# Bucketed attention and a feed-forward on one core: mask products over 64 rows, hashes in four column groups, squares on ScalarE, and weights converted in place

## The chip, the cores and the metric

The kernel runs on one core of a Trainium2 chip. Five engines work side by side, each with an instruction queue of its own that it takes in order: PE (TensorE, matrix products; PEld are its weight loads), DVE (VectorE), ACT (ScalarE), POOL (GpSimd) and SP (SyncE, which issues the DMAs here). They meet through semaphores. PE and the others exchange data through PSUM, which has eight banks for each partition; everything else lies in SBUF. The metric is device time in microseconds. Before the change the median of three runs is 1216.94 us (1216.66 to 1217.87).

## What is computed

```python
# q, k, v: (4, 8, 768, 64); proj: (64, 6)
q_bucket = sum of (q @ proj > 0) * 2**bit          # 6 bits a token
k_bucket = the same of k
mask = q_bucket[..., :, None] == k_bucket[..., None, :]
scores = where(mask, (q @ k.T) / 8, -1e9)
attn = softmax(scores); x = attn @ v               # (4, 8, 768, 64)
x = x.transpose(0, 2, 1, 3).reshape(3072, 512)
h = x @ w_in                                       # (512, 2048), float64 input
g = maximum(h, 0) + alpha * minimum(h, 0)
out = g @ w_out                                    # (2048, 512)
```

## The kernel before

There are two functions. `fast_path` computes everything on the assumption that exponents can't overflow, and writes a flag; `general_path` runs only if the flag says so. With this data it doesn't run, and it isn't changed.

`fast_path` works on **pairs** of heads: 4 batches of 4 pairs, the two heads of a pair side by side in the partitions 0 to 63 and 64 to 127. A **unit** is one pair and one half (384) of its queries, so there are 32 units, `u` = 0 to 31, and a unit has four **slots**. The scores are made transposed: a key tile of 128 keys by 384 queries for each head, six key tiles `kc` a unit, two in each of the slots 0, 2 and 3 (a **part**).

- `turn` transposes q and k of the next pair on PE (`tp_q`, `tp_k`), and ACT copies them to `qT`, `kT`. `magnitude` reduces those to a maximum and a minimum (`mags`, L548, DVE); `verdict` makes the flag of them at the end.
- `hash_bits` multiplies qT and kT by the projection (`hs`, L561, PE): q into the PSUM rows 0 to 63 and k into 64 to 127, each with the bits of both heads. Four DVE instructions a half (L565, L567) make of it the bit tiles `qb` and `kb`, 12 rows for each head: 6 bits and their complements, `kb` scaled so that their product is large and negative where the buckets differ.
- `scores` adds for each head that mask product (12 rows, bf16) and the product of qT and kT (64 rows, f32, which PE does in two passes) in PSUM (`sc`, L578). ACT makes exponentials of them (`pt`, L583), and the sum over the six key tiles is made in `acc` (L591): on POOL, and in the first batch for `kc` 4 and 5 on DVE.
- `attend` (slot 0 of the next unit) multiplies with v (`av`, L598); `divide` (slot 2) sums `acc` over its partitions with a product by ones (`sm`, L615) and divides: two DVE instructions (L619, L620), the reciprocal (L621), and on POOL a product (L622) and a sum (L623) into `xT`.
- The weights come as 8-byte floats. `round_weight` makes f32 of a block of 128 x 1024: ACT takes an absolute value (L521), DVE has five instructions (L522, L523, L526, L527, L530), between which ACT has another one (L528) and POOL an addition (L529). There are 16 blocks, two a unit in the units 0 to 7. The first feed-forward work (`h`, `neg`, `g`) belongs to unit 9 by the program.
- The feed-forward of a batch (`ff1`: `h`, L632, and `neg`, `g` on DVE; `ff2`: `z`, L648) is cut into the slots of the eight units that follow the batch's attention.

The program is written as one loop over units and slots, but the order of each engine's queue is set by a scheduler that goes by its own estimate of when each operand is ready, so an instruction can stand far from its place in the program. PSUM tiles named `sc`, `mi` and `ff` have two buffers each.

Of the kernel before, what the change touches and what calls it, by code (L numbers as in the profile page):

```python
# [348 lines left out]
def kernel(  # L349
# [31 lines left out]
    flag = const_flag = None  # L381
# [10 lines left out]
def fast_path(  # L392
# [12 lines left out]
    nc = tc.nc  # L405
# [15 lines left out]
    SAFE = 80.0 / SCALE / D  # L421
# [5 lines left out]
    psum = ctx.enter_context(tc.tile_pool(name="ps", bufs=2, space=bass.MemoryType.PSUM))  # L427

# [7 lines left out]
    wh = const.tile([P, D], F32, name="wh")  # L436
# [5 lines left out]
    mags = const.tile([P, 2, 2 * NPAIR], F32, name="mags")  # L442
# [3 lines left out]
    NPT = 9  # L446
# [4 lines left out]
    prob, acc, av, vmean, xT = {}, {}, {}, {}, {}  # L451

    def load(pi, names):
        b, hp = pairs[pi]
        for name, src in names:
            if name == "v":
                t = pool.tile([P, 2, NC * D], F32, name=f"vn{pi}", tag="vn", bufs=3)
                nc.sync.dma_start(t, src[b, 2 * hp : 2 * hp + 2].rearrange("h (p c) d -> p h (c d)", c=NC))
            else:
                t = pool.tile([P, NC, 2, D], F32, name=f"{name}n{pi}", tag=f"{name}n")  # L460
                for s in range(2):
                    nc.sync.dma_start(t[:, :, s], src[b, 2 * hp + s].rearrange("(p c) d -> p c d", c=NC))
# [8 lines left out]
    def setup():  # L471


        nc.vector.memset(wh, 0.0)
        for s in range(2):
            nc.sync.dma_start(wh[D * s : D * s + D, 32 * s : 32 * s + NB], proj)
# [3 lines left out]
        for s in range(2):  # L480
            r = slice(D * s, D * s + D)
            nc.vector.tensor_copy(wh[r, 32 * s + NB : 32 * s + 2 * NB], wh[r, 32 * s : 32 * s + NB])
        for t, inner, outer in ((cq, 0.5, 0.0), (tk, 0.0, -3.0e38), (mk, 2.0 * BIG, -BIG)):
            nc.vector.memset(t, 0.0)
            for r in range(0, P, 32):
                nc.vector.memset(t[r : r + 2 * NB], outer)
                nc.vector.memset(t[r : r + NB], inner)
        for t in pts:
# [11 lines left out]
    def load_weight(i):  # L500
        dst, src, j = views[i // 2]
        half = i % 2
        if src is moe_w_in:
            w = DFF // 4
            view = src[half * DM // 2 : (half + 1) * DM // 2, j * w : (j + 1) * w]
        else:
            w = DFF // 8
            view = src[(2 * j + half) * w : (2 * j + half + 1) * w]
        raw[i] = wpool.tile([P, 2, 512], src.dtype, name=f"raw{i}", tag="raw")
        nc.sync.dma_start(raw[i], view.rearrange("(o p) f -> p o f", p=P))  # L510

    def round_weight(i):
# [3 lines left out]
        words = raw[i].bitcast(U32).rearrange("p o (f t) -> p o f t", t=2)  # L516
        lo, hi = words[:, :, :, 0], words[:, :, :, 1]
        dst = views[i // 2][0][:, 2 * (i % 2) : 2 * (i % 2) + 2]
        x = wpool.tile([P, 2, 512], F32, name=f"wx{i}", tag="wx")
        r = wpool.tile([P, 2, 512], F32, name=f"wr{i}", tag="wr")  # L520
        nc.scalar.activation(x, hi.bitcast(F32), AF.Abs)  # L521
        nc.vector.tensor_scalar(x, x, HI_MIN, HI_MAX, op0=ALU.max, op1=ALU.min)  # L522
        nc.vector.tensor_scalar(  # L523
            x.bitcast(U32), x.bitcast(U32), 3, 0x40000000, op0=ALU.logical_shift_left, op1=ALU.bitwise_xor,
        )
        nc.vector.tensor_scalar(r.bitcast(U32), x.bitcast(U32), 0x7F800000, None, op0=ALU.bitwise_and)  # L526
        nc.vector.scalar_tensor_tensor(r, lo, 2.0 ** -52, r, op0=ALU.mult, op1=ALU.mult)  # L527
        nc.scalar.activation(x, x, AF.Abs)  # L528
        nc.gpsimd.tensor_tensor(r, x, r, op=ALU.add)  # L529
# [5 lines left out]
    def turn(pi, name, half):  # L535
# [4 lines left out]
        for i in range(CH):  # L540
            nc.tensor.transpose(ps[:, i * P : (i + 1) * P], src[:, CH * half + i], ident)  # L541
        nc.scalar.copy(tr[name, pi][:, half * CW : (half + 1) * CW], ps)  # L542

    def magnitude(pi, name):

        n = "qk".index(name)
        for i, op in enumerate((ALU.max, ALU.min)):
            nc.vector.tensor_reduce(  # L548
                mags[:, n, 2 * pi + i : 2 * pi + i + 1], tr[name, pi], axis=mybir.AxisListType.X, op=op,
            )  # L550

    def hash_bits(pi, half):


        if half == 0:
            for name in "qk":
# [232 lines left out]
```

## Time and profile before

| | |
|---|---|
| median of the runs | 1216.94 us |
| the profiled execution | 1216.79 us, span 1215.0 us |
| PE busy | 1132.4 us (93%) |
| DVE busy | 527.1 us (43%) |
| POOL busy | 364.3 us (30%) |
| ACT busy | 243.3 us (20%) |
| mean granted clock of PE | 0.956 |
| longest PE groups | `h` 344.3 us, `z` 339.0 us, `sc` product 188.8 us, `av` 142.4 us |

Shares of the whole span hide that the stages differ. The page's slices, each a fortieth of the span, and the busy times by stage show where which engine is full. A row of a group gives the line, the engine, the operation, what it writes and reads, partitions x elements, the count, the busy time, the mean length of one, and the idle time of the engine just before them with what ended it. PE's matrix products are pipelined, so the length of one says less than the distance between two starts.

### The profile page before, as it was taken

The page shows a single profiled execution, that of the slowest core. Times are in us where ns is not written, and L with a number is a line of the kernel's source. Part 1 is how long each engine was busy: PE and PEld are TensorE (multiplying, and loading weights), DVE is VectorE, ACT ScalarE, POOL GpSimd, SP SyncE. Part 2 cuts the span into 40 slices and gives each one's busy share as a digit, 9 for nine tenths or more (in the row PEclk, how much of TensorE's full clock was granted, in tenths as well). Part 3 has the DMA queues.
Part 4 walks back from the last instruction along what each step waited for, and adds up shares of the span by engine and source line. Part 5 has one row for each costly group of instructions (what it writes and reads, how often), then busy time and mean ns, then how long its engine had stood idle before and what let it go on. Part 6 is the DMA issues. An engine that isn't in the chain of part 4 may idle for free.

```text
span 1215.0 us, 10348 instructions
## 1 busy us (share of the span) xinstructions
PE 1132.4 (93%) x4163; PEld 503.5 (41%) x4163; DVE 527.1 (43%) x697; ACT 243.3 (20%) x345; POOL 364.3 (30%) x239
## 2 busy tenths in 40 slices
PE   7576765999999999999999999999999999999998
PEld 3122221344444444444444444444444444554553
DVE  7889888564313442164313442164313431330320
ACT  4443433222111121212121221222121111000000
POOL 3455556433222332333222332333223331000000
PEclk8777887799999999999999999999999999999999
DMA  7432332101010101000010101000000000000000
GB/s 195 127 124 82 109 96 83 26 13 26 22 35 22 26 13 35 18 13 27 22 35 22 26 13 35 18 14 14 9 9 9 1 1 18 9 1 18 9 9 20
DMA packets 62585, 42.72 MB, mean 35 GB/s; under 512 B 51248, under 2 KB 55360, under 8 KB 62528
## 3 DMA queue, kind: packets, MB, share of 16 engines
q1 hardware_dynamic: 62528, 41.96, 11.9%
q8 instruction: 35, 0.57, 0.2%
q14 instruction: 22, 0.18, 0.1%
HBM read 35.66 MB, written 6.29 MB: 35 GB/s over the span
## 4 chain that ended last, share of the span: by engine, by line
PE 84%; DVE 9%; POOL 3%; issue 3%; ACT 1%; DMA 0%; POOLq 0%; ACTq 0%
PE z L648 28%; PE h L632 27%; PE sc L578 14%; PE av L598 9%; POOL wr L529 3%; PE hs L561 2%; PE sm L615 2%; DVE wx L523 1%; DVE wr L527 1%; DVE wx L522 1%; DVE w_in L530 1%; PE tp_q L541 1%; PE tp_k L541 1%; DVE kb L567 1%; DVE w_out L530 1%
## 5 line engine op out<-in xcount | busy, mean ns | idle before, releaser
L632 PE MATMUL h<-xT,w_in 128*128 128x384 f32 x1024 | 344.3, 489 | 0.0
L648 PE MATMUL z<-w_out,g 128*128 128x512 f32 x768 | 339.0, 595 | 0.0
L591 POOL TENSOR_TENSOR acc<-acc,pt 128x768 f32<-128x768 f32 x112 | 193.6, 1729 | 447.2 <-ACT pt L583 444.0
L632 PEld LDWEIGHTS h<-xT,w_in 128*128 128x128 f32 x1024 | 189.4, 190 | 136.8 <-issue 14.8
L583 ACT ACTIVATE pt<-sc 128x768 f32<-128x768 f32 x192 | 154.9, 811 | 450.3 <-PE sc L578 450.3
L648 PEld LDWEIGHTS z<-w_out,g 128*128 128x128 f32 x768 | 143.2, 190 | 179.4 <-issue 177.3
L637 DVE TENSOR_SCALAR neg<-h,alpha 128x384 f32<-128x384 f32 x128 | 79.1, 618 | 275.0 <-PE h L632 273.0
L578 PE MATMUL sc<-qT,kT 64*128 64x384 f32 x768 | 188.8, 561 | 0.0
L598 PE MATMUL av<-pt,vn 128*64 128x385 f32 x768 | 142.4, 521 | 24.2 <-DVE dn L620 24.2
L578 PE MATMUL sc<-qb,kb 12*128 12x384 bf16 x384 | 70.7, 344 | 38.6 <-DVE kb L567 31.6
L598 PEld LDWEIGHTS av<-pt,vn 128*64 128x64 f32 x768 | 55.6, 146 | 108.9 <-issue 83.0
L591 POOL TENSOR_TENSOR acc<-pt,pt 128x768 f32<-128x768 f32 x32 | 59.3, 1853 | 120.6 <-ACT pt L583 120.6
L578 PEld LDWEIGHTS <-kb 12*128 12x128 bf16 x384 | 19.3, 92 | 152.7 <-issue 117.7
L619 DVE TENSOR_SCALAR al<-sm,vm 128x384 f32<-128x384 f32 x32 | 19.8, 617 | 144.1 <-PE sm L615 143.9
L621 DVE RECIPROCAL dn<-dn 128x384 f32<-128x384 f32 x32 | 81.6, 2551 | 0.9
L578 PEld LDWEIGHTS sc<-qT,kT 64*128 64x128 f32 x768 | 61.5, 193 | 36.0 <-issue 36.0
L548 DVE TENSOR_REDUCE mags<-qT 128x1 f32<-128x768 f32 x32 | 29.2, 945 | 101.5 <-ACT qT L542 101.5
L639 DVE SCALAR_TENSOR_TENSOR g<-h,neg 128x384 f32<-128x384 f32 x128 | 71.2, 556 | 3.9
L654 ACT COPY o<-z 128x512 f32<-128x512 f32 x24 | 14.0, 585 | 265.9 <-PE z L648 265.9
L622 POOL TENSOR_TENSOR dn<-rx,dn 128x384 f32<-128x384 f32 x32 | 36.1, 1128 | 71.8 <-DVE dn L621 71.7
L529 POOL TENSOR_TENSOR wr<-wx,wr 128x1024 f32<-128x1024 f32 x16 | 43.1, 2695 | 37.2 <-DVE wr L527 29.7
L565 DVE TENSOR_SCALAR qb<-hs,cq 12x384 bf16<-12x384 f32 x64 | 37.7, 590 | 37.6 <-PE hs L561 37.1
(59 smaller groups left out, 507.4 us busy)
## 6 DMA issues: line engine op xcount, KB each, us to landing
raw<-in_moe_w_in_dram SPq DMA_DIRECT2D x8, 1024.0 KB, 5.1
raw<-in_moe_w_out_dram SPq DMA_DIRECT2D x8, 1024.0 KB, 4.8
qn<-in_q_dram SPq DMA_DIRECT2D x32, 192.0 KB, 3.9
kn<-in_k_dram SPq DMA_DIRECT2D x32, 192.0 KB, 3.3
vn<-in_v_dram SPq DMA_DIRECT2D x16, 384.0 KB, 3.4
out_dram<-o SPq DMA_DIRECT2D x24, 256.0 KB, 2.0
wh<-in_proj_dram SPq DMA_DIRECT2D x2, 1.5 KB, 3.2
alpha<-in_moe_alpha_dram SPq DMA_DIRECT2D x1, 8.0 KB, 2.5
```

The costliest lines, as they stand in the source:

```text
L529: nc.gpsimd.tensor_tensor(r, x, r, op=ALU.add)
L565: nc.vector.tensor_scalar(bits["q", pi][dst, cols], ps[r], 0.0, cq[r], op0=ALU.is_gt, op1=ALU.subtract)
L578: nc.tensor.matmul(sc[:, s, :CW], what["k", pi][r, ks], what["q", pi][r, qs], start=first, stop=not first,)
L583: nc.scalar.activation(pt[:, :, :CW], sc[:, :, :CW], AF.Exp, scale=SCALE)
L591: eng.tensor_tensor(a, first, pt[:, :, :CW], op=ALU.add)
L598: nc.tensor.matmul(ps[D * s : D * s + D], nat["v", pi][:, s, kc * D : (kc + 1) * D], prob[pi, g, kc][:, s], start=(kc == 0), stop=(kc == N ...
L621: nc.vector.reciprocal(den, den)
L622: nc.gpsimd.tensor_tensor(den, av[pi, g], den, op=ALU.mult)
L632: nc.tensor.matmul(ps, w[:, kk, o : o + P], xT[b][:, kk, ch * CW : (ch + 1) * CW], start=(kk == 0), stop=(kk == NK - 1),)
L637: nc.vector.tensor_scalar(neg, ps, 0.0, alpha[:, f : f + 1], op0=ALU.min, op1=ALU.mult)
L639: nc.vector.scalar_tensor_tensor(g, ps, 0.0, neg, op0=ALU.max, op1=ALU.add)
L648: nc.tensor.matmul(ps, gT[b, ch, f][:, t * P : (t + 1) * P], w_out[part][:, i], start=(f == 0), stop=(f == NF - 1),)
```

## The change

- The bit tiles are zero outside their 12 rows, and the mask product takes 64 rows for each head.
- The hash is made in four column groups of 32 PSUM rows: head 0 q, head 0 k, head 1 q, head 1 k, with two projections `wh` of 32 columns. `qb` is then made in one DVE instruction over 128 rows, `kb` in two over 32 rows. `kb` has two fixed buffers, zeroed once.
- `magnitude` is a Square on ACT with a running sum, in place on the q or k tile, instead of two DVE reductions; the flag's bound is changed to suit.
- Weights are converted in 32 quarters of 128 x 512, in place in `w_in` and `w_out`, with one buffer `wr` and three raw tiles. By the loop there are two quarters a unit in the units 0 to 6 and four a unit from unit 7.
- In the first batch `acc` is three tiles, each the POOL sum of two key tiles, and `divide` adds them with three products by ones. Later batches keep the chain, all of it on POOL.
- `attend` copies into `xT`; the product of the division is on DVE in place of POOL.
- q and k have one buffer each, v two, `pt` eight; the loads of q, k and v are issued later and one by one. The pool of the feed-forward is opened at the start.
- Every product is pinned to program order on PE (`pe`).

```diff
+    pe = tc.keep_in_program_order
-    wh = const.tile([P, D], F32, name="wh")
+    wh = [const.tile([P, 32], F32, name=f"wh{s}") for s in range(2)]
+    kbs = [const.tile([P, S], BF16, name=f"kb{i}") for i in range(2)]
-    NPT = 9
+    NPT = 8
...
     def load_weight(i):
-        raw[i] = wpool.tile([P, 2, 512], src.dtype, name=f"raw{i}", tag="raw")
-        nc.sync.dma_start(raw[i], view.rearrange("(o p) f -> p o f", p=P))
+        raw[i] = wpool.tile([P, 512], src.dtype, name=f"raw{i}", tag="raw", bufs=3)
+        nc.sync.dma_start(raw[i], view)
...
     def round_weight(i):
-        x = wpool.tile([P, 2, 512], F32, name=f"wx{i}", tag="wx")
-        r = wpool.tile([P, 2, 512], F32, name=f"wr{i}", tag="wr")
-        nc.scalar.activation(x, hi.bitcast(F32), AF.Abs)
-        nc.vector.tensor_scalar(x, x, HI_MIN, HI_MAX, op0=ALU.max, op1=ALU.min)
+        r = wpool.tile([P, 512], F32, name=f"wr{i}", tag="wr", bufs=1)
+        nc.scalar.activation(dst, hi.bitcast(F32), AF.Abs)
+        nc.vector.tensor_scalar(dst, dst, HI_MIN, HI_MAX, op0=ALU.max, op1=ALU.min)
...
     def magnitude(pi, name):
-        for i, op in enumerate((ALU.max, ALU.min)):
-            nc.vector.tensor_reduce(
-                mags[:, n, 2 * pi + i : 2 * pi + i + 1], tr[name, pi], axis=mybir.AxisListType.X, op=op,
-            )
+        t = nat[name, pi].rearrange("p c h d -> p (c h d)")
+        nc.scalar.activation(t, t, AF.Square, accum_out=mags[:, n, pi : pi + 1])
     def hash_bits(pi, half):
-        for n, name in enumerate("qk"):
-            nc.tensor.matmul(ps[D * n : D * n + D], wh, tr[name, pi][:, cols], start=True, stop=True)
         for s in range(2):
-            dst = slice(D * s, D * s + 2 * NB)
-            r = slice(32 * s, 32 * s + 2 * NB)
-            nc.vector.tensor_scalar(bits["q", pi][dst, cols], ps[r], 0.0, cq[r], op0=ALU.is_gt, op1=ALU.subtract)
-            r = slice(D + 32 * s, D + 32 * s + 2 * NB)
-            nc.vector.tensor_scalar(bits["k", pi][dst, cols], ps[r], tk[r], mk[r], op0=ALU.is_gt, op1=ALU.mult)
+            for n, name in enumerate("qk"):
+                r = D * s + 32 * n
+                pe(nc.tensor.matmul(ps[r : r + 32], wh[s], tr[name, pi][:, cols], start=True, stop=True))
+        nc.vector.tensor_scalar(bits["q", pi][:, cols], ps, tq, cq, op0=ALU.is_gt, op1=ALU.subtract)
+        for s in range(2):
+            r = slice(D * s + 32, D * s + D)
+            nc.vector.tensor_scalar(
+                bits["k", pi][D * s : D * s + 32, cols], ps[r], tk[r], mk[r], op0=ALU.is_gt, op1=ALU.mult,
+            )
     def scores(pi, g, part):
-            for what, first, rows in ((bits, True, 2 * NB), (tr, False, D)):
+            for what, first in ((bits, True), (tr, False)):
                 for s in range(2):
-                    r = slice(D * s, D * s + rows)
+                    r = slice(D * s, D * s + D)
...
-                eng = nc.vector if pi < NP and kc >= 4 else nc.gpsimd
-                eng.tensor_tensor(a, first, pt[:, :, :CW], op=ALU.add)
+            if kc % 2 == 0 and (kc == 0 or pi < NP):
+                acc.setdefault((pi, g), []).append(pool.tile([P, 2, CW], F32, name=f"acc{pi}_{g}_{kc}", tag="acc", bufs=4))
+            a = acc[pi, g][-1]
+            if kc == 1 or (pi < NP and kc % 2 == 1):
+                nc.gpsimd.tensor_tensor(a, prob[pi, g, kc - 1][:, :, :CW], pt[:, :, :CW], op=ALU.add)
+            elif pi >= NP and kc > 1:
+                nc.gpsimd.tensor_tensor(a, a, pt[:, :, :CW], op=ALU.add)
     def divide(pi, g):
-        for s in range(2):
-            nc.tensor.matmul(ps[D * s : D * s + D], ones, acc[pi, g][:, s], start=True, stop=True)
+        n = len(acc[pi, g])
+        for i, a in enumerate(acc[pi, g]):
+            for s in range(2):
+                pe(nc.tensor.matmul(ps[D * s : D * s + D], ones, a[:, s], start=(i == 0), stop=(i == n - 1)))
...
-        nc.gpsimd.tensor_tensor(den, av[pi, g], den, op=ALU.mult)
+        nc.vector.tensor_tensor(den, den, x, op=ALU.mult)
...
-            if slot % 2 == 0 and 2 * u + slot // 2 < NW:
-                i = 2 * u + slot // 2
+            i = 2 * u + slot // 2 if u < UNITS - 1 else 4 * u + slot - 2 * UNITS + 2
+            if (slot % 2 == 0 or u >= UNITS - 1) and i < NW:
                 round_weight(i)
-                if i + 2 < NW:
-                    load_weight(i + 2)
+                if i + 3 < NW:
+                    load_weight(i + 3)
```

The order of the queues shows what the scheduler makes of it. The rows below have the line, the instruction, what it writes and reads with the tile's number, and the shape. In the changed kernel the lines of a conversion are L531, L532, L535, L536 and L539, in the order of L522 to L530.

DVE in the second pair, before, two blocks of weights after the hash bits:

```order
L567 TENSOR_SCALAR kb_614<-hs_646,tk,mk 12x384
L522 TENSOR_SCALAR wx_675<-wx_675 128x1024
L522 TENSOR_SCALAR wx_727<-wx_727 128x1024
L523 TENSOR_SCALAR wx_675<-wx_675 128x1024
L523 TENSOR_SCALAR wx_727<-wx_727 128x1024
L526 TENSOR_SCALAR wr_676<-wx_675 128x1024
L526 TENSOR_SCALAR wr_728<-wx_727 128x1024
L527 SCALAR_TENSOR_TENSOR wr_676<-raw_555,wr_676 128x1024
L527 SCALAR_TENSOR_TENSOR wr_728<-raw_609,wr_728 128x1024
L530 SCALAR_TENSOR_TENSOR w_out_81<-raw_555,wr_676 128x1024
L548 TENSOR_REDUCE mags<-qT_687 128x1
```

and at the same place of the changed kernel, with quarters:

```order
L535 TENSOR_SCALAR wr_1051<-w_in_84 128x512
L532 TENSOR_SCALAR w_out_85<-w_out_85 128x512
L536 SCALAR_TENSOR_TENSOR wr_1051<-raw_918,wr_1051 128x512
L531 TENSOR_SCALAR w_out_85<-w_out_85 128x512
L532 TENSOR_SCALAR w_out_85<-w_out_85 128x512
L539 SCALAR_TENSOR_TENSOR w_in_84<-raw_918,wr_1051 128x512
L535 TENSOR_SCALAR wr_1081<-w_out_85 128x512
L536 SCALAR_TENSOR_TENSOR wr_1081<-raw_970,wr_1081 128x512
L539 SCALAR_TENSOR_TENSOR w_out_85<-raw_970,wr_1081 128x512
L535 TENSOR_SCALAR wr_1130<-w_out_85 128x512
L536 SCALAR_TENSOR_TENSOR wr_1130<-raw_1027,wr_1130 128x512
L539 SCALAR_TENSOR_TENSOR w_out_85<-raw_1027,wr_1130 128x512
```

Two blocks went abreast through two `wx` and two `wr`; now one quarter follows another through one `wr`, and L539 often stands right behind L536.

DVE of the changed kernel where the conversion ends; `al`, `dn` and `den` belong to the division of the last unit of the first batch, `neg` and `g` to the feed-forward:

```order
L532 TENSOR_SCALAR w_out_88<-w_out_88 128x512
L535 TENSOR_SCALAR wr_1733<-w_out_88 128x512
L536 SCALAR_TENSOR_TENSOR wr_1733<-raw_1604,wr_1733 128x512
L539 SCALAR_TENSOR_TENSOR w_out_88<-raw_1604,wr_1733 128x512
L630 TENSOR_SCALAR al_1_1249<-sm_1_1241,vm_1048 128x384
L631 TENSOR_SCALAR dn_1_1248<-sm_1_1241 128x384
L632 RECIPROCAL dn_1_1248<-dn_1_1248 128x384
L633 TENSOR_TENSOR dn_1_1248<-dn_1_1248,xT_344 128x384
L648 TENSOR_SCALAR neg_0_0_1319<-h_0_0_1314,alpha 128x384
L650 SCALAR_TENSOR_TENSOR g_0_0_1321<-h_0_0_1314,neg_0_0_1319 128x384
```

The last of the 32 quarters stands ahead of the first `neg`, though by the loop the quarters run on into the units with feed-forward.

PE in unit 9, before, where the hash of the next pair stands between scores and feed-forward:

```order
L578 MATMUL sc_1_3_1285<-qb_1077,kb_1078 128x384
L578 MATMUL sc_1_3_1285<-qT_921,kT_1023 128x384 x2
L561 MATMUL hs_1296<-qT_1143,wh 64x384
L561 MATMUL hs_1296<-kT_1223,wh 64x384
L632 MATMUL h_0_3_1303<-xT_387,w_in_77 128x384 x4
L632 MATMUL h_0_4_1312<-xT_387,w_in_78 128x384 x4
L615 MATMUL sm_0_1322<-acc_0_1133,ones 64x384 x2
```

and in the changed kernel:

```order
L587 MATMUL sc_1_3_1381<-qb_1093,kb_79 128x384
L587 MATMUL sc_1_3_1381<-qT_920,kT_1029 128x384 x2
L570 MATMUL hs_1401<-qT_1177,wh_70 32x384
L570 MATMUL hs_1401<-kT_1308,wh_70 32x384
L570 MATMUL hs_1401<-qT_1177,wh_71 32x384
L570 MATMUL hs_1401<-kT_1308,wh_71 32x384
L643 MATMUL h_0_3_1409<-xT_344,w_in_81 128x384 x4
L643 MATMUL h_0_4_1418<-xT_344,w_in_82 128x384 x4
L626 MATMUL sm_0_1427<-acc_0_0_1158,ones 64x384 x2
```

The neighbours are the same, and the hash has four products in place of two.

## What I predicted before the run

> **What bounds the kernel now.** I read the page's slices first, then the busy times by stage, then the DVE groups of the first stage and the PE timeline of the second. Four lines of the page:
>
> ```profile
> span 1215.0 us, 10348 instructions
> ...
> PE   7576765999999999999999999999999999999998
> ...
> DVE  7889888564313442164313442164313431330320
> ...
> PEclk8777887799999999999999999999999999999999
> ```
>
> There are two kernels in one: some eight slices in which DVE is fuller than PE and the granted clock is low, and then PE filled to the end. The busy times by stage (length, then PE, PEld, DVE, ACT, POOL with counts, granted clock, DMA share, GB/s) put the border at 238.3 us, where the feed-forward (`h`) begins in earnest:
>
> ```profile
> 17.60:210.60 193.00, 129.42 (x562) 47.15 (x560) 166.84 (x155) 78.45 (x101) 105.76 (x51) 0.78 0.35 106
> 210.60:238.30 27.70, 22.66 (x90) 8.01 (x91) 17.73 (x21) 7.30 (x11) 12.18 (x8) 0.69 0.11 28
> 238.30:1208.30 970.00, 970.00 (x3482) 443.86 (x3481) 331.77 (x479) 151.98 (x226) 245.43 (x166) 1.00 0.06 17
> ```
>
> From 17.6 to 238.3 us (220.7 us) DVE works 166.84 + 17.73 = 184.6 us and rests 36.1. From 238.3 on PE is busy for 970.00 of 970.00 us at clock 1.00. So two things can shorten the program: less DVE work, or fewer DVE waits, ahead of 238.3; and less time on PE behind it. DVE's groups from 17.6 to 238.3 us (line, engine, operation, shapes, count, busy us, mean ns, idle before):
>
> ```profile
> L527 DVE SCALAR_TENSOR_TENSOR wr<-raw,wr 128x1024 f32<-128x1024 uint32 x16 | 22.2, 1400 | 0.1
> ...
> L530 DVE SCALAR_TENSOR_TENSOR w_in<-raw,wr 128x1024 uint32<-128x1024 uint32 x8 | 19.6, 2457 | 13.8 <-POOL wr L529 13.8
> L530 DVE SCALAR_TENSOR_TENSOR w_out<-raw,wr 128x1024 uint32<-128x1024 uint32 x8 | 18.8, 2353 | 12.3 <-POOL wr L529 12.3
> L523 DVE TENSOR_SCALAR wx<-wx 128x1024 uint32<-128x1024 uint32 x16 | 18.4, 1166 | 0.1
> L522 DVE TENSOR_SCALAR wx<-wx 128x1024 f32<-128x1024 f32 x16 | 17.1, 1081 | 1.3 <-ACT wx L521 1.2
> L591 DVE TENSOR_TENSOR acc<-acc,pt 128x768 f32<-128x768 f32 x16 | 16.3, 1020 | 0.0
> L526 DVE TENSOR_SCALAR wr<-wx 128x1024 uint32<-128x1024 uint32 x16 | 12.2, 778 | 0.1
> L567 DVE TENSOR_SCALAR kb<-hs,tk,mk 12x384 bf16<-12x384 f32 x16 | 10.9, 680 | 0.3
> L565 DVE TENSOR_SCALAR qb<-hs,cq 12x384 bf16<-12x384 f32 x16 | 9.7, 603 | 0.2
> L548 DVE TENSOR_REDUCE mags<-qT 128x1 f32<-128x768 f32 x10 | 9.2, 940 | 7.1 <-ACT qT L542 7.1
> L548 DVE TENSOR_REDUCE mags<-kT 128x1 f32<-128x768 f32 x8 | 7.4, 941 | 0.0
> ```
>
> The conversion of the weights (L522 to L530) is 108.3 us of it. Its two L530 rows also hold 13.8 + 12.3 = 26.1 us of the 36.1 us of rest: DVE waits there for the POOL addition (L529).
>
> **Stage 1: the conversion isn't spread.** The loop asks for two quarter conversions in each of the units 0 to 6 and four afterwards, which would halve DVE's load in the first batch. The order of instructions says otherwise: DVE's rows are not pinned, and all 32 quarters stand ahead of the first `neg` of the feed-forward, some four between one division and the next. So the 108.3 us stay in stage 1. I cost the edits there one by one.
>
> Removed from DVE: the additions into `acc`, 16.3 us, and the `mags` reductions, 9.2 + 7.4 = 16.6 us. The hash bits take three instructions a half where they took four: 20.6 us become 8 halves x (0.60 + 2 x 0.68) = 15.7, so -4.9; I take 128 or 32 rows to cost what 12 rows do, since all have 384 columns. Added: the product in the division moves from POOL to DVE, 8 x 0.51 = 4.1 us (half of an L591 instruction of 1020 ns, which has twice the columns); and 160 conversion instructions of 512 columns in place of 80 of 1024. No row shows how much of an instruction is fixed. The bounds are 0 and 0.1 us each; I take 0.06 x 80 = 4.8. DVE's work is then 184.6 - 16.3 - 16.6 - 4.9 + 4.1 + 4.8 = **155.7 us**.
>
> ```profile
> L529 POOL TENSOR_TENSOR wr<-wx,wr 128x1024 f32<-128x1024 f32 x16 | 43.1, 2695 | 37.2 <-DVE wr L527 29.7 <-ACT pt L583 7.5
> ...
> L632 PE MATMUL h<-xT,w_in 128*128 128x384 f32 x13 | 5.2, 510 | 0.0
> ```
>
> Its rest: `wr` has one buffer now, so the next quarter can't enter it until the last instruction of this one (L539, which was L530) has read it, and that one waits for POOL's addition, 2695 / 2 = 1.35 us. There are twice as many waits of half the length. In some the order puts the next quarter's first two instructions or hash bits, in about half it puts nothing. Bounds: 18 us (half the waits gone) and 62 (all 32 additions fully exposed, 32 x 1.6, and 10 of other rest). I keep the 36.1 of now.
>
> The first conversion starts when the first raw tile has landed; its Abs starts at 16.45 us now:
>
> ```profile
> 16.45 1.11 ACT L521 ACTIVATE wx<-raw 128x1024 f32<-128x1024 f32 x1
> ```
>
> The tile is half as large, so I put the first DVE conversion at 15.5 us instead of 17.6 (bounds 12.5 and 17.6). The feed-forward then begins at 15.5 + 155.7 + 36.1 = 207 us instead of 238.3: **-31 us** (bounds -52 and -3).
>
> What else moves in stage 1 I cost at nothing, for a named cover. The page's group for the Exp:
>
> ```profile
> L583 ACT ACTIVATE pt<-sc 128x768 f32<-128x768 f32 x192 | 154.9, 811 | 450.3 <-PE sc L578 450.3
> ```
>  Two more `sm` pairs in 8 units on PE lie in its 193.00 - 129.42 = 63.6 us of rest. Square on ACT, 10 times about 0.81 us like an Exp over as large a tile, lies in ACT's rest of 193.00 - 78.45 = 114.6 us. The q and k loads with one buffer wait behind Square, but are issued more than a unit ahead of their transposes; only the pair 1 load at the very start is late, where DVE isn't waiting for it. One thing is given back: the scheduler slipped early pieces of `h` into PE's rest, the 13 records above, of which 12 belong to three pieces ahead of their turn. With PE pinned to program order they are paid in stage 2: 12 x 0.33 = **+4 us**. If the cover on PE failed, that is the last rival below.
>
> **Stage 2: the scores.** PE's timeline (start us, us, instruction); a unit issues three such parts of two key tiles each:
>
> ```profile
> 401.41 0.34 PE L578 MATMUL sc<-qb,kb 12*128 12x384 bf16 x2
> 401.67 0.92 PE L578 MATMUL sc<-qT,kT 64*128 64x384 f32 x4
> 402.52 0.34 PE L578 MATMUL sc<-qb,kb 12*128 12x384 bf16 x2
> 402.79 0.92 PE L578 MATMUL sc<-qT,kT 64*128 64x384 f32 x4
> 403.63 0.55 PE L541 MATMUL tp_q<-ident,qn 128*128 128x128 f32 x3
> ...
> 406.69 4.10 PE L598 MATMUL av<-pt,vn 128*64 128x385 f32 x24
> 410.72 0.55 PE L541 MATMUL tp_q<-ident,qn 128*128 128x128 f32 x3
> 411.11 5.33 PE L632 MATMUL h<-xT,w_in 128*128 128x384 f32 x16
> 416.37 0.34 PE L578 MATMUL sc<-qb,kb 12*128 12x384 bf16 x2
> ```
>
> Read starts, not lengths. The two heads run side by side, on different rows of the array. The mask pair takes 401.67 - 401.41 = 0.26 us to the next start, the two product passes 0.85: a part is 403.63 - 401.41 = 2.22 us. In an unbroken stream a pass of 384 columns takes (416.37 - 411.11) / 16 = 0.33 us, and a pair side by side (410.72 - 406.69) / 12 = 0.34. So two passes should take 0.65, not 0.85. A bf16 pass is shorter than an f32 pass by the difference of their lengths:
>
> ```profile
> L632 PE MATMUL h<-xT,w_in 128*128 128x384 f32 x1012 | 339.7, 489 | 0.0
> ...
> L578 PE MATMUL sc<-qb,kb 12*128 12x384 bf16 x272 | 45.6, 332 | 0.0
> ```
>
> 489 - 332 = 157 ns, so 0.33 - 0.16 = 0.17 us, not 0.26. A key tile pays 0.09 + 0.20 = 0.29 us on top of its streaming, wherever the rows used change between 12 and 64. With 64 rows in both the shape no longer changes within a part, and only the change at its end (0.09) stays: 2 x (0.17 + 0.65) + 0.09 = 1.73 us, 0.49 less. 272 mask records are 68 parts behind 238.3 us: 68 x 0.49 = **-33 us** (bounds 0, if none of the 0.29 hangs on the shape, and -39, if the change at the end costs nothing either). The zero rows add no time, since a pass goes by columns.
>
> The Trainium skill, "TensorEngine Tiling (Array Packing)", section "Key Properties", says that a change of the tiling mode drains the TensorE. The trace agrees: the two f32 passes take 0.84 us to the f32 transpose, which uses 128 rows (402.79 to 403.63), as they take 0.85 to the mask. By that rule the sum is as given. A rule speaks against: "TensorE: Matmul & The Clock Gate", section "The mechanism", lets a weight load overlap a running matmul only when the row groups differ. By that, loads of the same rows stay exposed and the part keeps its 2.22 us. The `h` stream speaks against so strict a reading: its loads use the same 128 rows each time, and its passes follow each other at 0.33 us. This is the rival B below.
>
> **Stage 2: the hash.** Two column groups now, four after, twice the instructions:
>
> ```profile
> 450.36 0.54 PE L561 MATMUL hs<-qT,wh 128*64 128x384 f32 x1
> 450.37 0.54 PE L561 MATMUL hs<-kT,wh 128*64 128x384 f32 x1
> 450.74 0.49 PE L561 MATMUL hs<-qT,wh 128*64 128x384 f32 x1
> 450.74 0.49 PE L561 MATMUL hs<-kT,wh 128*64 128x384 f32 x1
> 451.16 7.13 PE L648 MATMUL z<-w_out,g 128*128 128x512 f32 x16
> ```
>
> Both groups start within 0.01 us, and a half costs 451.16 - 450.36 = 0.80 us. Four groups cost the same if all start together, and two passes more (0.65) if only pairs do. There are 22 halves behind 238.3: bounds 0 and +14. I take 0, by the nearest row. The rest of PE's order in stage 2 is the same as before. DVE loses reductions there and gains a product; it works 331.77 of 970 us and hides both.
>
> **The sum.** The profiled execution took 1216.8 us (span 1215.0), the median of the runs 1216.94. 1216.8 - 31 - 33 + 4 = **1157 us**.
>
> **Rivals.**
> - B, the surcharge isn't of the shape but of the type (bf16 next to f32) or of the weight load: the trace holds no mask and product with the same rows to exclude it. 1157 + 33 = 1190.
> - C, stage 1 keeps its length: the single `wr` buffer and raw tiles fetched in smaller lead make DVE wait as much as it saves; all 32 additions exposed make almost that. 1157 + 31 = 1188.
> - E, DVE's rest halves because quarters interleave better, and the start is early: 1157 - 21 = 1136.
> - D, slower: PE can't leave its program order in stage 1, waits for hash bits, and its clock stays at half. A unit's PE work at full clock is 3 x 1.73 + 4.0 + 0.8 (transposes) + 0.8 + 3 x 0.8 = 13.2 us, at half 26.4. Nine units of 26.4 and the start of 15 make 253; it is slower than before once stage 1 exceeds 238.3 + 33 - 4 = 267, that is units over 28 us, half clock throughout and over 1.7 us of waiting each. At 4 us of waiting: 15 + 9 x 30.4 = 289, 1157 + (289 - 207) = 1239. Against it: the clock was 0.78 with PE busy in two thirds of the stage.
> - B and C together: 1221, a little slower.
>
> **How the numbers follow.** The forecast 1157 gets 0.58, B 0.12, C 0.13, E 0.07; in all these it is faster, 0.90. D gets 0.05 and B with C 0.02: slower 0.07. Partial forms of B and C that cancel: same, 0.03. "Same" is within 0.2%, about what a measurement of this kernel can tell. The range 1134 to 1192 takes in the bounds of stage 1 below, B and C above, and leaves out D and B with C.
>
> **What would show it.** In the changed profile: `h` in earnest from 207 us; DVE without `mags` reductions and `acc`, rest near 36 us ahead of that point; from mask to product 0.17 us and a part of 1.73; four `hs` starts within 0.03 us and 0.80 to what follows; clock 1.00 in stage 2 with PE never resting. It would be wrong if the mask pair still takes 0.26, if the idle time of DVE before L539 doubles, if the hash takes 1.4, or if PE's clock in stage 1 falls under 0.7.

## The result, and the profile after

The changed kernel takes **1161.81 us** in the median of four runs (1160.29 to 1164.71), beside 1216.93 us before (1216.66 to 1217.87): a ratio of 0.955 (95% interval 0.953 to 0.957), 55 us faster. The forecast was 1157, the range 1134 to 1192. The profiled execution took 1162.11 us. The page's span, three of its rows by slices:

```profile
span 1160.3 us, 10928 instructions
...
PE   5676675999999999999999999999999999999997
...
DVE  5988988444325430354315430354315421420420
...
PEclk8888787999999999999999999999999999999999
```

DVE is fuller than PE in the slices 2 to 7, as it was before, and from the eighth on PE is as full as before. A slice is 29.0 us (30.4 before), too coarse to show how far the border moved. The busy times by stage have the same columns as in the prediction (length, PE, PEld, DVE, ACT, POOL, granted clock, DMA share, GB/s). The border is now at 214.0 us, where `h` begins in earnest. The first row is of before, cut at 238.3; the other two are of the changed kernel:

```profile
17.00:238.30 221.30, 152.67 (x654) 55.16 (x651) 184.57 (x174) 86.31 (x113) 117.93 (x59) 0.77 0.32 97
```

```profile
15.00:214.00 199.00, 137.23 (x733) 59.05 (x734) 165.86 (x219) 96.59 (x163) 101.15 (x68) 0.84 0.37 105
...
214.00:1153.70 939.70, 939.70 (x3582) 447.49 (x3581) 320.44 (x437) 169.79 (x268) 222.33 (x141) 1.00 0.07 19
```

The first stage gave 238.3 - 214.0 = 24 us, the second 970.0 - 939.7 = 30 us. In the first, DVE works 165.9 us and rests 199.0 - 165.9 = 33.1 us; forecast were 155.7 and 36.1. In the second PE is still busy for all of it at clock 1.00.

**Scores and hash in the second stage.** PE's timeline of the changed kernel (start, length, instruction):

```profile
226.39 0.34 PE L587 MATMUL sc<-qb,kb 64*128 64x384 bf16 x2
226.56 0.81 PE L587 MATMUL sc<-qT,kT 64*128 64x384 f32 x4
227.21 0.33 PE L587 MATMUL sc<-qb,kb 64*128 64x384 bf16 x2
227.37 0.81 PE L587 MATMUL sc<-qT,kT 64*128 64x384 f32 x4
228.11 0.51 PE L570 MATMUL hs<-qT,wh 128*32 128x384 f32 x1
228.12 0.51 PE L570 MATMUL hs<-kT,wh 128*32 128x384 f32 x1
228.12 0.51 PE L570 MATMUL hs<-qT,wh 128*32 128x384 f32 x1
228.13 0.51 PE L570 MATMUL hs<-kT,wh 128*32 128x384 f32 x1
...
228.89 5.43 PE L643 MATMUL h<-xT,w_in 128*128 128x384 f32 x16
```

From mask to product it is 226.56 - 226.39 = 0.17 us (0.26 before), the two passes and the change to the next mask take 0.65, and the part 228.11 - 226.39 = 1.72 us (2.22 before, 1.73 forecast). All four hash groups start within 0.02 us, and a half costs 228.89 - 228.11 = 0.78 us, as with two groups.

**Where the first stage misses its forecast.** The conversion's costliest DVE groups from 15 to 214 us (count, busy us, mean ns, idle before):

```profile
L539 DVE SCALAR_TENSOR_TENSOR w_in<-raw,wr 128x512 uint32<-128x512 uint32 x16 | 19.1, 1193 | 9.2 <-POOL wr L538 9.0
L531 DVE TENSOR_SCALAR w_out<-w_out 128x512 f32<-128x512 f32 x16 | 16.9, 1053 | 1.9 <-ACT w_out L530 1.9
...
L539 DVE SCALAR_TENSOR_TENSOR w_out<-raw,wr 128x512 uint32<-128x512 uint32 x16 | 15.5, 971 | 10.4 <-POOL wr L538 10.3
L531 DVE TENSOR_SCALAR w_in<-w_in 128x512 f32<-128x512 f32 x15 | 14.8, 985 | 2.7 <-ACT w_in L530 2.7
...
L535 DVE TENSOR_SCALAR wr<-w_in 128x512 uint32<-128x512 uint32 x16 | 6.8, 424 | 0.4
```

L531 and L535 are the same kind of instruction on tiles of one size, and one takes about 1000 ns, the other 424. A mean hides two kinds here. Three neighbours of DVE and what POOL did at that time, from the two timelines:

```profile
126.01 1.23 DVE L531 TENSOR_SCALAR w_out<-w_out 128x512 f32<-128x512 f32 x1
...
128.09 1.50 DVE L531 TENSOR_SCALAR w_out<-w_out 128x512 f32<-128x512 f32 x1
129.51 2.29 DVE L539 SCALAR_TENSOR_TENSOR w_out<-raw,wr 128x512 uint32<-128x512 uint32 x1
```

```profile
125.83 1.12 POOL L634 TENSOR_TENSOR xT<-dn,al 128x384 f32<-128x384 f32 x1 [1.58 <-DVE dn L633]
128.00 1.30 POOL L538 TENSOR_TENSOR wr<-w_out,wr 128x512 f32<-128x512 f32 x1 [1.05 <-DVE wr L536]
129.27 1.99 POOL L599 TENSOR_TENSOR acc<-pt,pt 128x768 f32<-128x768 f32 x1
```

Each of the three starts while a POOL instruction runs. POOL's end at 126.95, 129.30 and 131.26; DVE's end at 127.24, 129.59 and 131.80, that is 0.29, 0.29 and 0.54 us later, however long they overlapped. In the whole stage 35 of the conversion's instructions are stretched so: 27 of L531 and L532 end 0.28 to 0.29 us behind POOL's instruction, 8 of L539 0.55 us behind it. Those that meet no POOL instruction take 0.42 (L531, L532) and 0.69 us (L539). The 22 that start ahead of POOL's instruction and overlap it keep these lengths. POOL's additions of 512 columns take 1.26 to 1.30 us with and without DVE beside them. Together the 35 are 41 us longer than they would be alone. The reciprocals and the readers of PSUM (L574) overlap POOL too and are not longer.

The Trainium skill, "SBUF — State Buffer", section "Who interferes with whom", has the rule for it: DVE instructions in a two-port mode or with two SBUF inputs share a port pair with GpSimd, and the one that comes second blocks until the first is done. The rows agree: the end of DVE's hangs on POOL's end and not on the overlap. L531 and L532 have one input each; in which mode they run, no trace here shows. What the rule costs here, the experiments show.

### The profile page after: what moved, and what is told of

The parts are those of the page before. It is cut to its first block, busy times and chain, and to the rows that moved or that the text cites. A ratio compares the mean times of both kernels' runs of the same rounds, so it can differ in the third digit from the quotient of the medians.

```text
span 1160.3 us, 10928 instructions
## 1 busy us (share of the span) xinstructions
PE 1084.9 (94%) x4355; PEld 510.7 (44%) x4355; DVE 492.9 (42%) x696; ACT 272.9 (24%) x441; POOL 325.8 (28%) x224
## 4 chain that ended last, share of the span: by engine, by line
PE 82%; DVE 13%; POOL 2%; ACT 1%; issue 1%; DMA 1%; SPq 0%; POOLq 0%; ACTq 0%
PE h L643 29%; PE z L659 29%; PE sc L587 10%; PE av L608 9%; PE sm L626 2%; DVE w_in L539 2%; POOL wr L538 2%; DVE dn L632 1%; PE hs L570 1%; DVE w_out L531 1%; DVE wr L536 1%; DVE w_out L539 1%; DVE w_in L531 1%; DVE wr L535 1%; DVE kb L574 1%; PE tp_k L550 1%
## 5 line engine op out<-in xcount | busy, mean ns | idle before, releaser
L601 POOL TENSOR_TENSOR acc<-acc,pt 128x768 f32<-128x768 f32 x96 | 161.0, 1677 | 427.2 <-ACT pt L592 423.4
L587 PE MATMUL sc<-qT,kT 64*128 64x384 f32 x768 | 160.7, 497 | 0.0
L599 POOL TENSOR_TENSOR acc<-pt,pt 128x768 f32<-128x768 f32 x48 | 89.9, 1874 | 116.5 <-ACT pt L592 116.5
L587 PE MATMUL sc<-qb,kb 64*128 64x384 bf16 x384 | 65.2, 335 | 18.5 <-ACT pt L592 18.4
L587 PEld LDWEIGHTS sc<-qT,kT 64*128 64x128 f32 x768 | 71.1, 195 | 20.5 <-issue 20.4
L587 PEld LDWEIGHTS <-kb 64*128 64x128 bf16 x384 | 20.5, 94 | 91.2 <-issue 78.5
L570 PE MATMUL hs<-qT,wh 128*32 128x384 f32 x128 | 30.4, 555 | 23.3 <-ACT xT L618 22.6
L618 ACT COPY xT<-av 128x384 f32<-128x384 f32 x32 | 15.2, 474 | 155.9 <-PE av L608 83.4
L634 POOL TENSOR_TENSOR xT<-dn,al 128x384 f32<-128x384 f32 x32 | 32.2, 1007 | 56.3 <-DVE dn L633 56.3
L626 PE MATMUL sm<-acc,ones 128*64 128x384 f32 x192 | 44.1, 574 | 1.2 <-ACT xT L618 1.2
```

The lines of the kernel that those rows point to most:

```text
L570: pe(nc.tensor.matmul(ps[r : r + 32], wh[s], tr[name, pi][:, cols], start=True, stop=True))
L587: pe(nc.tensor.matmul(sc[:, s, :CW], what["k", pi][r, ks], what["q", pi][r, qs], start=first, stop=not first,))
L599: nc.gpsimd.tensor_tensor(a, prob[pi, g, kc - 1][:, :, :CW], pt[:, :, :CW], op=ALU.add)
L601: nc.gpsimd.tensor_tensor(a, a, pt[:, :, :CW], op=ALU.add)
L626: pe(nc.tensor.matmul(ps[D * s : D * s + D], ones, a[:, s], start=(i == 0), stop=(i == n - 1)))
```

## The experiments

All ratios are to the kernel before on the same chip. Line numbers of experiments can be shifted by one to three.

### Which rows cost: four sizes of the mask product

The theory was the prediction's: the surcharge hangs on the change between 12 and 64 rows. In three kernels the changed kernel's mask product takes fewer rows of the same tiles; the rows that it leaves out are zero.

```diff
-            for what, first in ((bits, True), (tr, False)):
+            for what, first, rows in ((bits, True, 2 * NB), (tr, False, D)):   # 12; then 32; then 40
                 for s in range(2):
-                    r = slice(D * s, D * s + D)
+                    r = slice(D * s, D * s + rows)
```

12 rows:

> The changed kernel with its mask product over 12 rows again; the product passes keep 64. Theory (the surcharge hangs on the change between 12 and 64 rows): in the feed-forward stage the start of a product comes 0.26 us after that of its mask instead of 0.16, a part takes 2.2 us instead of 1.70, 68 parts by 0.49 give 33 us, so about 1195 us. Rival (the surcharge goes because the bits are zero-padded, pinned or laid out otherwise, not because of the rows used): 1162 us and 0.16 us. The first stage should stay at about 214 us under both.

32 rows:

> The same over 32 rows. If any change in the number of rows between mask and product costs, or if only 64 rows escape: 0.26 us from mask to product and about 1195 us, as with 12 rows. If the cost grows with the difference in rows (52 rows with 12, 32 with 32, none with 64): about 0.22 us and 1182 us.

40 rows:

> The same over 40 rows. If what counts is the number of rows rounded up to a group of 32, 64 or 128: 0.16 us from mask to product and 1162 us, as with 64 rows. If every difference in rows costs: 0.26 us and about 1195 us. If the cost grows with the difference: about 0.21 us and 1177 us.

And the kernel before with only this part: two zeroed bit tiles each for q and k, and 64 rows in the mask product.

```diff
+    bts = {(n, i): const.tile([P, S], BF16, name=f"{n}b{i}") for n in "qk" for i in range(2)}
-                bits[name, pi] = pool.tile([P, S], BF16, name=f"{name}b{pi}", tag=f"{name}b")
+                bits[name, pi] = bts[name, pi % 2]
-            for what, first, rows in ((bits, True, 2 * NB), (tr, False, D)):
+            for what, first, rows in ((bits, True, D), (tr, False, D)):
```

> The kernel before with this part of the change alone: bit tiles that are zeroed once, and mask products over 64 rows. Theory: the feed-forward stage falls from 970.0 by 33 to about 937 us and the first stage keeps its 238 us: 1217 - 33 = 1184 us. Rival (the part gains only together with the program order that the change pins on TensorE): under 10 us gained, over 1207 us.

Measured, with two runs each: 12 rows **1197.99** us (ratio 0.985 [0.980, 0.990]), 32 rows **1196.26** (0.983 [0.978, 0.989]), 40 rows **1161.60** (0.955 [0.950, 0.960]), before with 64 rows **1174.67** (0.966 [0.961, 0.970]). PE's timeline with 12 rows, then with 32 and with 40:

```profile
405.24 0.34 PE L587 MATMUL sc<-qb,kb 12*128 12x384 bf16 x2
405.51 0.92 PE L587 MATMUL sc<-qT,kT 64*128 64x384 f32 x4
406.36 0.34 PE L587 MATMUL sc<-qb,kb 12*128 12x384 bf16 x2
...
407.47 4.78 PE L643 MATMUL h<-xT,w_in 128*128 128x384 f32 x14
```

```profile
213.00 0.34 PE L587 MATMUL sc<-qb,kb 32*128 32x384 bf16 x2
213.26 0.92 PE L587 MATMUL sc<-qT,kT 64*128 64x384 f32 x4
214.11 0.34 PE L587 MATMUL sc<-qb,kb 32*128 32x384 bf16 x2
```

```profile
401.86 0.34 PE L587 MATMUL sc<-qb,kb 40*128 40x384 bf16 x2
402.03 0.81 PE L587 MATMUL sc<-qT,kT 64*128 64x384 f32 x4
402.68 0.33 PE L587 MATMUL sc<-qb,kb 40*128 40x384 bf16 x2
```

With 12 rows a mask takes 0.27 us and its product 0.85 again (0.26 and 0.85 before), with 32 rows 0.26 and 0.85, and 40 rows behave like 64. With 12 rows the second stage takes 974.1 us, 34.4 more than in the changed kernel. So neither type, padding nor pinning is the cause, nor any difference in rows as such: somewhere above 32 and up to 40 rows the mask product falls into the group of the 64-row product. Rival B is out. The Trainium skill, "TensorEngine Tiling (Array Packing)", section "Available Configurations", lists tilings of 32, 64 and 128 rows; that 40 rows count as 64 agrees with it.

The kernel before gained 42 us, not 33. Its second stage gave 34, as forecast, and its first 8 more:

```profile
17.00:230.30 213.30, 132.97 (x651) 58.40 (x651) 185.14 (x174) 85.82 (x114) 117.77 (x58) 0.79 0.33 101
230.30:1166.00 935.70, 935.70 (x3482) 446.70 (x3481) 331.53 (x479) 151.63 (x226) 246.49 (x167) 1.00 0.06 18
```

DVE works as long there (185.1 against 184.6 us), but rests 28 us instead of 37. PE is 20 us less busy, which probably made DVE wait less; no run separates that. In the changed kernel it isn't repeated: with 12 rows `h` starts at 215.0 instead of 214.0.

### What the first stage pays for

Four changes of the changed kernel. First the clamp L531 pinned to program order, so that conversions lie in both batches:

```diff
-        nc.vector.tensor_scalar(dst, dst, HI_MIN, HI_MAX, op0=ALU.max, op1=ALU.min)
+        pe(nc.vector.tensor_scalar(dst, dst, HI_MIN, HI_MAX, op0=ALU.max, op1=ALU.min))
```

> The changed kernel with the first clamp of each quarter (L531) pinned to program order on VectorE, so that the conversions really lie where the loop asks for them, over both batches. Theory (the first stage is bound by VectorE, and the conversion is most of its work there; moved behind the first feed-forward blocks it is hidden under TensorE): the feed-forward begins at 170 to 185 us, TensorE may wait a few us for a late quarter, 1120 to 1135 us. Rival 1 (the first stage is bound by something else by now, the loads or TensorE at its reduced clock): under 10 us gained, over 1152. Rival 2 (pinning makes VectorE's other work wait behind clamps whose tile has not landed): 1162 or more.

The magnitudes back on DVE:

```diff
-        nc.scalar.activation(t, t, AF.Square, accum_out=mags[:, n, pi : pi + 1])
+        for m, op in ((mags, ALU.max), (lows, ALU.min)):
+            nc.vector.tensor_reduce(m[:, n, pi : pi + 1], tr[name, pi], axis=mybir.AxisListType.X, op=op)
```

> The changed kernel with the magnitudes taken by two reductions on VectorE again, in place of the square on ScalarE (the flag's bound is then made of maxima). Theory (each us of VectorE's work ahead of the feed-forward is paid): 16.6 us more of it in the first stage, the feed-forward begins at about 230 us, 1178 us. Rival (VectorE has rest to take them in): 1162 to 1166.

The first batch's sums of exponentials off POOL, as products on PE:

```diff
+            if pi < NP:
+                acc.setdefault((pi, g), []).append(pt[:, :, :CW])
+                continue
...
                     attend(*before)
+                    if before[0] < NP:
+                        divide(*before)
...
-                if slot == 2:
+                if slot == 2 and before[0] >= NP:
                     divide(*before)
```

> The changed kernel without GpSimd's additions of exponentials in the first batch; the products with ones take all six tiles of a half instead of three sums, and the division follows at once. Theory (VectorE's conversions take two to four times as long while GpSimd runs, since both use one path to the memory; 42 us of VectorE's 166 us between 15 and 214 us are such excess, and about half of GpSimd's work there are these additions): 15 to 20 us less VectorE time, the feed-forward begins at 195 to 200 us, 3 us more on TensorE behind it, 1146 to 1150 us. Rival (the excess is of the conversions' own waits or of their operands, whatever GpSimd does): the groups' means stay within 10% and the time is 1160 to 1166 us.

PE's order left to the scheduler:

```diff
-    pe = tc.keep_in_program_order
+    pe = lambda ins: ins
```

> The changed kernel with TensorE's rows left to the scheduler, as they were before the change. Theory (the early pieces of the feed-forward are slipped into TensorE's rest again, which was 4 us, and nothing else depends on the order): 1158 us. Rival 1 (the pinning keeps the hash and the transposes ahead of waiting products, so that without it VectorE starves): the feed-forward begins later than 220 us, over 1168. Rival 2: no difference, within 2 us of 1162.

| | median us | ratio to before | `h` starts, us | DVE works / rests ahead of it, from 15 us |
|---|---|---|---|---|
| the changed kernel | 1161.81 | 0.955 [0.953, 0.957] | 214.0 | 165.9 / 33.1 |
| clamps pinned | 1166.35 | 0.957 [0.955, 0.960] | in pieces | 145.4 / 59.6 (to 220) |
| magnitudes on DVE | 1167.77 | 0.960 [0.958, 0.961] | 219.8 | 179.6 / 25.1 |
| no sums on POOL | 1147.93 | 0.944 [0.942, 0.945] | 199.3 | 140.0 / 44.3 |
| PE not pinned | 1165.20 | 0.957 [0.954, 0.959] | 216.8 | 168.4 / 33.4 |

*No sums on POOL* came out as the lock theory said. POOL is busy 53.8 us of the stage instead of 101, and the conversion's stretched instructions fall from 35 to 17, their excess from 41 to 14 us, while the lengths of undisturbed ones stay (the first row is the stage, the other two are L539):

```profile
15.00:199.30 184.30, 141.31 (x829) 66.53 (x830) 139.98 (x219) 96.53 (x162) 53.81 (x43) 0.92 0.38 113
```

```profile
L539 DVE SCALAR_TENSOR_TENSOR w_out<-raw,wr 128x512 uint32<-128x512 uint32 x16 | 12.5, 784 | 7.7 <-POOL wr L538 7.7
L539 DVE SCALAR_TENSOR_TENSOR w_in<-raw,wr 128x512 uint32<-128x512 uint32 x16 | 10.9, 683 | 10.3 <-POOL wr L538 10.3
```

The 25.9 us less DVE work are about the 27 us of excess that went. Two other things differ in this run: the division comes two slots earlier, and PE's granted clock is 0.92 (0.84 in the changed kernel). What these are worth wasn't separated. And 25.9 us less DVE work moved `h` by 14.7 us only: the rest grew by 11. *Magnitudes on DVE* shows the same from the other side. 13.8 us more work cost 5.8 us ahead of `h` and 6.0 in all, where 16.6 were expected; the rest took in 8. The time lies nearer the rival (1162 to 1166) than the theory (1178). A microsecond of DVE work is worth some 0.4 to 0.6 us here, not 1.

*Clamps pinned* was a miss. Its time is that of rival 2, but not for rival 2's reason: DVE rests only 0.1 us ahead of the clamps. The work ahead of 220 us fell, but the rest nearly doubled; two of DVE's groups from 15 to 260 us:

```profile
L539 DVE SCALAR_TENSOR_TENSOR w_in<-raw,wr 128x512 uint32<-128x512 uint32 x16 | 20.7, 1291 | 37.6 <-POOL wr L538 37.6
L539 DVE SCALAR_TENSOR_TENSOR w_out<-raw,wr 128x512 uint32<-128x512 uint32 x12 | 17.5, 1458 | 17.0 <-POOL wr L538 17.0
```

In program order nothing stands between a quarter's L536 and its L539, so DVE waits 54.6 us for POOL's additions, against 19.3 in the changed kernel, where the scheduler lets quarters interleave.

*PE not pinned* was 3 us slower by medians, the ranges overlap (1161.98 to 1165.59). That it would save the 4 us is refuted; no `h` is slipped in ahead of 216 us there either.

### Without POOL in the conversion

The addition L538 on DVE, alone and together with the sums on PE, and the latter with pinned clamps:

```diff
-        nc.gpsimd.tensor_tensor(r, dst, r, op=ALU.add)
+        nc.vector.tensor_tensor(r, dst, r, op=ALU.add)
```

> The changed kernel with the addition of each conversion (L538) on VectorE instead of GpSimd; GpSimd keeps the sums of exponentials. Theory (a VectorE instruction that meets a running GpSimd instruction ends 0.28 or 0.55 us after that one's end, so each of the 32 additions on GpSimd costs a wait or a stretched instruction): 32 additions of about 0.69 us are added to VectorE, 22 us; 19 us of waiting for GpSimd and about 12 us of stretching go. The feed-forward begins at about 205 us, 1153 us. Rival (the stretching goes with whatever GpSimd does and the sums of exponentials, which are longer, now meet the additions too): the same or slower, 1160 to 1172 us.

> Both together: no sums of exponentials on GpSimd in the first batch, and the conversions' additions on VectorE. From the run without the sums (1147.9): 16 us of stretching and 18 us of waiting for GpSimd go, 22 us are added, 1136 us, the feed-forward at 187 us, and no clamp or shift longer than 0.5 us. Rival (by now TensorE, 141 of 184 us busy at clock 0.92, and the round trips between the engines set the first stage): 1143 to 1149 us.

> The same with the first clamp of each quarter pinned to program order, so that half of the conversions lie behind the first batch. Theory (the earlier run with pinned clamps lost because VectorE stood for 55 us before L539, waiting for GpSimd; without GpSimd in the conversion that wait is gone): VectorE has about 50 us less ahead of the feed-forward, TensorE sets the first stage, the feed-forward begins at 160 to 170 us, 1110 to 1122 us. Rival (the clamps in order wait for raw tiles or for ScalarE, and hold VectorE's other work up): 1136 us or more.

Measured: the addition alone **1144.93** us (0.940 [0.939, 0.942]), both **1128.70** (0.927 [0.926, 0.929]), both with pinned clamps **1152.80** (0.948 [0.946, 0.951]). The stage rows of the first two:

```profile
15.00:196.10 181.10, 132.78 (x734) 59.26 (x735) 171.66 (x244) 95.18 (x161) 63.04 (x36) 0.88 0.40 116
```

```profile
15.00:180.10 165.10, 133.66 (x829) 63.41 (x830) 148.28 (x252) 96.85 (x163) 12.90 (x11) 0.96 0.44 127
```

With the addition alone DVE works 5.8 us more ahead of `h` than in the changed kernel, and yet `h` comes 18 us earlier: the rest falls by 24, from 33.1 to 181.1 - 171.7 = 9.4 us, where 19 were expected. Twice as much was gained as expected, 17 us instead of 9. The larger part of the surplus is order: the last of the conversion stands behind the first `h` here.

```profile
196.07 2.98 PE L643 MATMUL h<-xT,w_in 128*128 128x384 f32 x8
```

```profile
200.90 2.25 DVE L539 SCALAR_TENSOR_TENSOR w_out<-raw,wr 128x512 uint32<-128x512 uint32 x1
```

DVE's conversion instructions behind 196.1 us add up to 5.8 us; with them its work is 177 us, about the 176 that were expected (165.9 + 22 - 12). With both, DVE works 148.3 us (146 expected) and rests 16.8, and the granted clock of PE is 0.96. Three clamps are still stretched, by 2.4 us together, where the expectation had none: POOL keeps the last addition of the division. This is **33 us faster than the changed kernel**, on the same work of PE in the second stage (180.1 to 1119.0, 938.9 us).

Pinned clamps lose here too, though no longer by waiting for POOL's addition. `h` starts at 190.4 us, in pieces. In program order the division stands ahead of the next quarter, and DVE waits for PE's sums (its groups from 15 to 300 us):

```profile
L633 DVE TENSOR_SCALAR al<-sm,vm 128x384 f32<-128x384 f32 x11 | 6.8, 616 | 37.8 <-PE sm L629 37.8
```

Without the pinning these waits are 14.7 us. And the quarters that now lie in the second batch meet POOL's sums of exponentials, which that batch keeps: up to 300 us the conversion is stretched by 20 us, beside 2.4 without the pinning. How the 24 us of loss divide between the two wasn't tried.

Last, how much of an instruction is fixed: the fastest kernel with blocks of 1024 columns, as before the change.

```diff
-        raw[i] = wpool.tile([P, 512], src.dtype, name=f"raw{i}", tag="raw", bufs=3)
+        raw[i] = wpool.tile([P, 2, 512], src.dtype, name=f"raw{i}", tag="raw", bufs=2)
-        r = wpool.tile([P, 512], F32, name=f"wr{i}", tag="wr", bufs=1)
+        r = wpool.tile([P, 2, 512], F32, name=f"wr{i}", tag="wr", bufs=1)
-            if (slot % 2 == 0 or u >= UNITS - 1) and i < NW:
-                round_weight(i)
+            if (slot % 2 == 0 or u >= UNITS - 1) and i < NW and i % 2 == 0:
+                round_weight(i // 2)
```

> The run without GpSimd in the first stage (1128.7 us) with the weights converted in blocks of 1024 columns again, 96 VectorE instructions instead of 192, two raw tiles of twice the size in place of three, and two tiles for the second batch's sums so that it fits. Theory (an instruction has a fixed part of about 0.15 us, read from means of 425 ns at 512 columns and 684 at 1024): 96 x 0.15 = 14 us less VectorE work, the first conversion 2 us later, the feed-forward at about 168 us, 1117 us, and means of about 0.69 us for the clamps and 1.22 for L539. Rival 1 (the fixed part is 0.06 us, as the prediction had it): 6 less and 2 later, 1125 us. Rival 2 (raw tiles fetched with less lead, or the longer blocks keep VectorE from the hash bits and TensorE waits): 1128 us or more.

Measured: **1127.13** us (0.925 [0.924, 0.927]), beside 1128.70: neither the theory nor rival 1, and within a microsecond or two of rival 2. The rows have the lengths that were expected, and the work is less, but `h` starts at 180.1 us all the same:

```profile
15.00:180.10 165.10, 136.92 (x830) 63.60 (x831) 139.70 (x156) 94.17 (x132) 13.77 (x11) 0.94 0.41 126
```

```profile
L540 DVE SCALAR_TENSOR_TENSOR w_in<-raw,wr 128x1024 uint32<-128x1024 uint32 x8 | 9.8, 1222 | 0.2
...
L532 DVE TENSOR_SCALAR w_in<-w_in 128x1024 f32<-128x1024 f32 x8 | 5.5, 683 | 5.1 <-ACT w_in L531 5.1
```

DVE's busy time is 148.3 - 139.7 = 8.6 us less for 96 instructions fewer, 0.09 us each. By their lengths DVE's instructions fell by 14.8 us, 0.15 each, as the theory had it (2 x 424 - 683 = 165 ns for a clamp); the other 6.2 us had been overlap of one instruction's end with the next one's start. The rest grows by the same 8.6 us (165.1 - 139.7 = 25.4 against 16.8) and takes the gain. By now the first stage isn't set by DVE's work alone: the last quarter is done at 157.0 us with 512 columns and at 153.7 with 1024, and from there to `h` PE is nearly full in both.

```profile
157.00:180.10 23.10, 21.27 (x143) 9.71 (x142) 12.63 (x15) 11.87 (x20) 6.25 (x5) 1.00 0.20 52
```

```profile
153.70:180.10 26.40, 25.19 (x169) 11.59 (x166) 12.74 (x15) 12.67 (x21) 6.32 (x5) 1.00 0.18 46
```

## Why the prediction was right, and where a term was off

- **Scores, -33 us net of 4: right.** The second stage gave 30.3 us, 29 were forecast. The part is 1.72 us (1.73), and the runs with 12, 32 and 40 rows show the cause. Rival B is out in both its forms: the type didn't change, and mask and product now load weights into the same rows and yet follow each other at 0.17 us. Against the run with 12 rows the scores are worth 34.4 us in the second stage, where 33 were forecast. Ahead of 238.3 us the sum gave them nothing; alone they gave 8 us there, in the changed kernel about 1.
- **Hash, 0: right**, within 0.02 us a half; DVE's part of it is in the first stage's sum.
- **Early `h`, +4: right in size, wrong in cause.** The changed kernel has none ahead of 214 us, and with 12 rows its second stage is 974.1 - 970.0 = 4.1 us longer than before. That the pinning did it is refuted: without it there are none either. What did stays open.
- **First stage, -31: it gave -24.** The first conversion starts at 14.4 us (15.5 forecast; the rows count from 15.0) and the rest is 33.1 (36.1); the step that failed is DVE's work, 165.9 us against 155.7 (158.9 with the upper bound of 0.1 us an instruction), and in it the term "0.06 x 80 = 4.8" for the conversion's halved blocks. The five instructions of the conversion took 108.3 us by their rows and take 124.6 now. The fixed part is one reason: 80 x 0.09 = 7 instead of 4.8. The other, which the sum didn't have at all, is the blocking by POOL. Counted in the same way, 30 of the 80 conversion instructions of before were stretched, by 37 us together; all but one ended 0.55 or 1.08 us behind POOL's, twice as late with twice the columns. With 35 and 41 us it grew by 4 where the sum, which scales the groups' means by size, had it unchanged. The two make 2 + 4 of the 10 us. The other 4 are overlaps with neighbours: the rows of `acc` and `mags` were taken off at their full 32.9 us, but without these instructions DVE's busy time in the trace of before is 155.5 instead of 184.6 us, 29.1 less. Part of the miss cancelled by luck: 10.2 us of work less 3.0 of rest and 0.5 of start make the 6.7 us between 207.3 and 214.0, and the second stage gave 1.3 more than forecast.
- **The rest as a constant: wrong as a rule, right by luck.** It was "kept" at 36.1 and came out at 33.1. The wait for POOL's addition in it fell from 26.1 to 19.3 us. In the variants the rest lay between 9 and 60 us. The rows of before pointed to POOL as the engine to free, by their 26 us of waiting for it and by means 1.4 to 1.7 times those of other instructions of the same size (L523 1166 ns beside L526 778, L530 2405 beside L527 1400); I read only the first of the two.
- **Rivals.** C (the first stage keeps its length) and E (the rest halves) did not occur; D (PE waits at half clock) neither, the clock rose from 0.77 to 0.84.

## What to carry to other kernels

When the same instruction on the same tile has a mean far above its shortest, look at what GpSimd does at that moment before trusting the mean, and count each GpSimd addition beside a VectorE-bound stage as VectorE time; here taking 32 additions of 1.3 us onto VectorE itself, at 0.69 us each, gained 17 us. Neighbouring products on TensorE should use the same group of rows: here 40 and 64 went together, and 12 and 32 did not go with 64. Zero rows cost nothing here: the mask takes 0.34 us with 12 rows and with 64. Busy time and idle time of the fullest engine are not two independent terms: a change of one comes back partly in the other.

## What was unexpected of the hardware

- A blocked VectorE instruction ends a fixed 0.28 us (one input, 512 columns) or 0.55 us (two inputs) behind GpSimd's, 0.14 us less than it takes alone, in all 35 cases of the changed kernel; GpSimd's own lengths hardly show the meeting (1.26 to 1.30 us).
- 40 rows of a product behave like 64, and 32 like 12, with a step of 0.29 us a key tile between them.
- The granted clock ahead of the feed-forward was 0.77 with PE busy in 69% of the stage in the kernel before, 0.84 in the changed kernel (69%), 0.92 without the sums on POOL (77%), 0.96 with the conversion's additions off POOL too (81%) and 0.94 with blocks of 1024 columns (83%). The share alone doesn't set it; what does, these runs don't show.
